# An attention and MLP kernel: h by Strassen's scheme over pairs of 384-token blocks, attention products in one group

## The chip, the core and the metric

The kernel runs on one core of a Trainium2 chip. Its engines are PE (TensorE, matrix products into PSUM), DVE (VectorE), ACT (ScalarE), POOL (GpSimd) and SP, whose queue issues every DMA here. The metric is device time in microseconds (us), the median of the runs shown.

## What is computed

Attention over 4 batches of 8 heads (576 tokens, head width 64) with a causal mask and a decay bias, then two MLPs over the 2304 tokens:

```python
attn = softmax(q @ k.T / 8 + min(-(cum_i - cum_j), 0), causal) @ v   # per batch and head
x = attn, heads side by side                       # (2304, 512)
a = x @ w1;  b = x @ w2                            # (512, 1024) each
x2 = ((a * b) @ w3) @ w_out                        # (1024, 1024), (1024, 512)
h = x2 @ w_in                                      # (512, 2048)
g = h - tanh(h)
out = g @ w_out2                                   # (2048, 512)
```

## The kernel before

Matrix products run in fp32r with every operand split into a high and a low part (`xh`, `xl`, `wih`, `wil`, ...): three matmuls (high x high, high x low, low x high) stand for one product. The split of a tile is a rounding copy (`copy`, L394 to L396, ACT or DVE) and a subtraction (`sub`, L398 to L401, DVE or POOL). The weights come as 64-bit floats in `wraw` and are put together by `assemble` (L490 to L502: one operation on ACT or DVE and four on DVE).

The program is a list of operations with the buffers that they read and write. A planner (`Plan.order`) runs this list through a model of the engines and writes the instructions of each engine in the order in which the model started them. Where an operation may run on two engines (`copy`: ACT or DVE; `sub`: DVE or POOL) it picks one. The numbers in `PARAM` are its priorities and biases, so a new `PARAM` is a new order everywhere. Engines and the SP queue run their lists strictly in order.

The stages follow each other on PE, with overlaps on the other engines:

- **Attention** (`head`, 32 heads). Scores of five query tiles into PSUM (L668 in batch 0, L670 and L671 later), the bias and row maximum on DVE (L685), the exponential on ACT (L691), transposes of the weights on PE into a ring of banks (`flip`, L725; from batch 1 on three banks, `tr_ring`), copies of these to `en`, and for a pair of heads the products with v (`pv`, L752) in two groups: query tiles 0 to 2 and tiles 3 to 4, into one bank (`pv_ring`), each followed by a copy to `xf`. `xf` is scaled by the inverse row sums (L780) and split into `xh`, `xl`.
- **Products** a and b over blocks of 512 tokens (`products`, L806), filler for PE between the heads; a times b (L815) goes to memory as `c_d`.
- **w3 times w_out** (L870 to L872), once, so that x2 needs one product.
- **x2** (L907 to L909): blocks `XT` of 512 tokens (four, and one of 256) are read back from `c_d`, split and multiplied; high and low parts go to memory as `x2_d`.
- **Last stage** (L926 to L978). For each of the five blocks `HT` and each of 16 slices f of w_in: twelve matmuls into one bank of a ring of four (h, L945), then the gate: Square, Square, Tanh, Relu on ACT (L953 to L958), four operations on DVE (L956, L957, L959, L960), a rounding copy `gh` and the residue `gl` (L401, POOL). One slice later come the output matmuls, three for each 128 tokens (L966 to L968), into four banks that collect all 16 slices. w_in is converted before the stage and stays in `wih` and `wil`.

```python
BLK = 512
HT = [(t, min(t + BLK, NT)) for t in range(0, NT, BLK)]
h_ring = Ring(bank[BLK // P:8])
s_ring.bufs, s_ring.i, tr_ring.bufs, tr_ring.i = bank[0:2], 0, bank[3:6], 0
```

## Time and profile before

| | us |
|---|---|
| median of 3 runs (930.68 to 930.79) | 930.7 |
| profiled execution | 931.5 |
| its span | 929.8 |
| busy: PE / DVE / ACT / POOL | 921.6 / 700.5 / 426.6 / 377.8 |
| attention with products, to 292 us | 292 |
| products and w3 x w_out | 142 |
| x2 | 98.5 |
| h, gate and output | 392.5 |
| tail | 4.8 |

Busy times are shares of one profiled execution. Matmuls are pipelined, and the profile models their ends: a PE that is busy throughout may still run below its rate, so the distance between the starts of matmuls is the better measure. The chain of waits follows the end of the program back from step to step; where it runs over PE, PE sets the time.

### The profile page before, as it was taken

The numbers are of one execution on the slowest core, as the hardware profiler recorded it, in microseconds if no ns is written. First come the engines' busy times: TensorE is split into PE (matmuls) and PEld (weight loads), VectorE is DVE, ScalarE is ACT, GpSimd is POOL, SyncE is SP. The second block draws the span as 40 slices with busy tenths as digits, with TensorE's granted clock in tenths as the row PEclk, the third lists the DMA queues.
The fourth block names the chain that finished last, engine by engine and source line by source line (L and its number), as shares of the span: only waits on it lengthen the run. The fifth ranks groups of instructions, "written<-read, shape, count | busy, mean of one in ns | idle before, by whom it ended". The sixth has DMA issues, their size and how long they took to land.

```text
span 929.8 us, 14217 instructions
## 1 busy us (share of the span) xinstructions
PE 921.6 (99%) x5007; PEld 765.1 (82%) x5007; DVE 700.5 (75%) x1485; ACT 426.6 (46%) x952; POOL 377.8 (41%) x309
## 2 busy tenths in 40 slices
PE   9999999999999999999999999999999999999998
PEld 7777878888887888899888988888888888888887
DVE  8999897876664299996789999997556655656665
ACT  7857565655551022211423275554444444444353
POOL 2256765545342044414978544452222222222221
PEclk9999999999999999999999999999999999999999
DMA  7666646654421144477897652221020001100010
GB/s 226 183 199 181 201 146 205 213 160 135 131 84 49 56 147 155 164 233 240 284 326 247 227 176 68 75 107 46 1 91 15 31 1 46 46 1 0 1 47 23
DMA packets 58888, 115.36 MB, mean 124 GB/s; under 512 B 5713, under 2 KB 24305, under 8 KB 58818
## 3 DMA queue, kind: packets, MB, share of 16 engines
q1 hardware_dynamic: 58818, 114.47, 38.6%
q8 instruction: 39, 0.64, 0.3%
q14 instruction: 31, 0.25, 0.1%
HBM read 85.30 MB, written 25.46 MB: 119 GB/s over the span
## 4 chain that ended last, share of the span: by engine, by line
PE 92%; DVE 4%; POOL 1%; issue 1%; ACT 1%; DMA 1%; POOLq 0%; DVEq 0%
PE bank L945 21%; PE bank L806 20%; PE bank L966 7%; PE bank L967 7%; PE bank L968 7%; PE bank L725 5%; PE bank L752 4%; PE bank L908 4%; PE bank L909 4%; PE bank L907 4%; PE bank L670 2%; PE bank L671 2%; PE bank L668 2%; PE bank L872 1%; PE bank L871 1%; PE bank L870 1%
## 5 line engine op out<-in xcount | busy, mean ns | idle before, releaser
L401 POOL TENSOR_TENSOR gl<-pg,gh 128x512 fp32r<-128x512 f32 (+1 forms) x78 | 99.2, 1272 | 260.9 <-DVE gh L396 249.0
L945 PE MATMUL bank<-x2b,wih 128*128 128x512 f32 (+1 forms) x640 | 181.3, 368 | 0.0
L945 PEld LDWEIGHTS bank<-x2b,wih 128*128 128x128 f32 x640 | 117.0, 188 | 21.2
L958 ACT ACTIVATE mk<-u,const 128x512 f32<-128x512 f32 (+1 forms) x80 | 54.5, 681 | 142.5 <-DVE pg L960 142.4
L945 PE MATMUL bank<-x2b,wil 128*128 128x512 f32 (+1 forms) x320 | 117.7, 368 | 0.0
L966 PE MATMUL bank<-voh,gh 128*128 128x512 f32 x288 | 112.2, 390 | 0.0
L967 PE MATMUL bank<-vol,gh 128*128 128x512 f32 x288 | 112.2, 390 | 0.0
L968 PE MATMUL bank<-voh,gl 128*128 128x512 f32 x288 | 112.0, 389 | 0.0
L691 ACT ACTIVATE e<-e,nmx 128x576 f32<-128x576 f32 (+4 forms) x160 | 89.2, 559 | 39.7 <-DVE nmx L685 38.8
L956 DVE TENSOR_TENSOR pg<-bank,u 128x512 f32<-128x512 f32 (+1 forms) x80 | 50.9, 636 | 42.3 <-POOL gl L401 42.3
L685 DVE CUSTOM_DVE_ANT_0 e<-bank,msk 128x288 f32<-128x288 f32 (+4 forms) x160 | 64.3, 422 | 16.5 <-PE bank L671 14.2
L725 PE MATMUL bank<-ident,e 128*128 128x128 f32 (+1 forms) x480 | 75.4, 276 | 0.6 <-ACT e L691 0.3
L396 DVE CAST gh<-pg 128x512 fp32r<-128x512 f32 (+1 forms) x77 | 30.5, 396 | 52.8 <-PE bank L967 52.6
L945 PEld LDWEIGHTS bank<-x2b,wil 128*128 128x128 f32 x320 | 60.3, 188 | 9.9
L401 POOL TENSOR_TENSOR xl<-cf,xh 128x512 fp32r<-128x512 f32 (+1 forms) x40 | 53.3, 1360 | 34.2 <-DVE xh L396 32.3
L953 ACT ACTIVATE u<-bank 128x512 f32<-128x512 f32 (+1 forms) x80 | 43.7, 546 | 50.4 <-PE bank L945 42.3
L395 ACT ACTIVATE en<-bank 128x256 f32<-128x256 f32 (+3 forms) x97 | 40.9, 427 | 52.2 <-PE bank L725 42.3
L495 ACT ACTIVATE wt<-wraw 128x512 f32<-128x512 f32 x54 | 36.4, 673 | 59.4 <-DMA wraw<-w_in 26.7
L968 PEld LDWEIGHTS bank<-voh,gl 128*128 128x128 f32 x288 | 54.1, 188 | 11.4
L966 PEld LDWEIGHTS bank<-voh,gh 128*128 128x128 f32 x288 | 54.2, 188 | 10.8
L967 PEld LDWEIGHTS bank<-vol,gh 128*128 128x128 f32 x288 | 54.1, 188 | 10.5
L806 PE MATMUL bank<-xh,w1h 128*128 128x512 f32 (+1 forms) x160 | 62.7, 392 | 0.0
(134 smaller groups left out, 2280.2 us busy)
## 6 DMA issues: line engine op xcount, KB each, us to landing
rqk<-qk SPq DMA_DIRECT2D x24, 576.0 KB
wraw<-w_out SPq DMA_DIRECT2D x24, 512.0 KB
wraw<-w SPq DMA_DIRECT2D x16, 512.0 KB
c_d<-cst SPq DMA_DIRECT2D x32, 256.0 KB
wraw<-w3t SPq DMA_DIRECT2D x16, 512.0 KB
wraw<-w_in SPq DMA_DIRECT2D x16, 512.0 KB
cf<-c_d SPq DMA_DIRECT2D x32, 256.0 KB
x_d<-x2s SPq DMA_DIRECT2D x16, 512.0 KB
```

Source lines behind the costliest of these rows:

```text
L401: o.append(("POOL", c_pool2(n), lambda: nc.gpsimd.tensor_tensor(dst(), a(), b().bitcast(F32), op=ALU.subtract)))
L685: nc.vector.tensor_tensor_reduce(e.t[:nq, EOFF[t] + k0:EOFF[t] + k1], bk.t[:nq, :k1 - k0], bi.t[:nq, bo + k0:bo + k1], -0.125, 3.0e38 if f ...
L691: act(lambda: nc.scalar.activation(et(), et(), AF.Exp, bias=nmx.t[:nq, i, tm:tm + 1], scale=-1.0, accum_out=ssum.t[:nq, pj, t, i:i + 1]), ...
L725: nc.tensor.transpose(bk.t[:rows, (at + m) * P:(at + m + 1) * P], e.t[:, EOFF[t] + c * P:EOFF[t] + c * P + rows], ident.t)
L806: nc.tensor.matmul(bk.t[:, :w], w_.t[:, k, f * P:(f + 1) * P], x_.t[:, k, :w], start=k == 0 and i == 0, stop=k == KC - 1 and i == 2)
L945: nc.tensor.matmul(bk.t[:, :w], w_.t[:, k, a], X2.t[:, i, k, :w], start=k == 0 and n == 0, stop=k == KC - 1 and n == 2)
L953: act(lambda u=u, hp=hp, c_=c_: nc.scalar.activation(c_(u), hp(), AF.Square), w, [bk], [u], pr, psum=True)
L956: dve(lambda u=u, pg=pg, hp=hp, c_=c_: nc.vector.tensor_tensor(c_(pg), hp(), c_(u), op=ALU.mult), w, [bk, u], [pg], pr)
L958: act(lambda u=u, mk=mk, c_=c_: nc.scalar.activation(c_(mk), c_(u), AF.Relu, bias=const.t[:, 1:2]), w, [u, const], [mk], pr, extra=93.0)
L966: nc.tensor.matmul(bank[n].t, gh.t[:, a], voh[f].t, start=f == 0, stop=False)
L967: nc.tensor.matmul(bank[n].t, gh.t[:, a], vol[f].t, start=False, stop=False)
L968: nc.tensor.matmul(bank[n].t, gl.t[:, a], voh[f].t, start=False, stop=f == NF2 - 1)
```

## The change

1. **h by Strassen's scheme** (Winograd's form). Tokens go in three pairs of 384-token blocks, w_in is cut into halves of its rows and of its columns. A step (one of 8 column slices, 128 columns of either half) makes the four products of the 2 x 2 scheme from seven: seven times six 384-column matmuls into two banks (three in the first pair's first step), and five additions on DVE out of these banks. m1, h11 and the rest then lie in SBUF, in the buffers `cst` and `asb`, and the gate reads them there.
2. **Its operands.** Combinations of w_in (`weights`) are made from a first conversion to memory (`wi_d`, laid by during the attention), split and written to `ws_d`; a step reads its seven of 256 kB each into a ring of 13. Combinations of x2 (`operands`) are made directly from the first two x2 blocks for the first pair, and through memory (`xf_d`, `x2_d`) for the later ones.
3. **x2** runs in six blocks of 384.
4. **Attention from batch 1 on:** both `pv` groups of a pair as one, in banks 2 and 3; the transposes have banks 4 and 5.
5. **A new `PARAM`**, and biases of its own for the planner near the end and for some kinds of operation. The output banks are six (3 x 128 tokens for two blocks).

```diff
-BLK = 512
-HT = [(t, min(t + BLK, NT)) for t in range(0, NT, BLK)]
-XT = [(t, min(t + 512, NT)) for t in range(0, NT, 512)]
+XB = 384
+XT = [(t, t + XB) for t in range(0, NT, XB)]
+NPAIR = len(XT) // 2
+NFP = NF2 // 2
+ORDER = (0, 5, 1, 6, 4, 3, 2)
...
-            s_ring.bufs, s_ring.i, tr_ring.bufs, tr_ring.i = bank[0:2], 0, bank[3:6], 0
+            s_ring.bufs, s_ring.i, tr_ring.bufs, tr_ring.i = bank[0:2], 0, bank[4:6], 0
+            pv_ring.bufs, pv_ring.i = bank[2:4], 0
...
+    for n in range(NF2):
+        c, kg, m = n // 8, n // 4 % 2, n % 4
+        j, i = ((0, 0), (0, 1), (1, 1), (1, 0))[m]
+        k, qd = j * 2 + kg, c + 2 * i
+        lay_by(wi_d, k * 4 + qd, w_in[k * P:(k + 1) * P, qd * 512:(qd + 1) * 512], PARAM["layw"] + 10 * n)
...
             if i:
-                pv(1)
+                pv([0, 1] if merged else [1])
...
+        def lay(i, x):
+            for m in range(2):
+                st = wst_r.next()
+                split(lambda st=st: st.t[:, :, 0], (st, 0), lambda st=st: st.t[:, :, 1], (st, 1),
+                      lambda m=m: v_(x).rearrange("p (f x) -> p f x", x=P)[:, m * 2:m * 2 + 2], 256, [x], pr, kind="late")
...
+            s3 = made(a11, a21)
+            lay(6, s3)
...
+        b11, b12, b21, b22 = b
+        lay(0, b11)
+        lay(1, b21)
+        lay(2, b22)
+        lay(4, made(b12, b11, b11))
+        lay(6, made(b22, b12, b12))
+        t2 = made(b22, b11)
+        lay(5, t2)
+        lay(3, made(b21, t2, b21))
...
+        def product(n, i, bk, first):
+            def mm():
+                for kg in range(2):
+                    for m, (a, z) in enumerate(((0, 0), (0, 1), (1, 0))):
+                        nc.tensor.matmul(bk.t[:, :XB], W[i].t[:, kg, a], X[i].t[:, kg, z], start=first and kg == 0 and m == 0, stop=kg == 1 and m == 2, skip_group_check=True)
...
+        def plus(bk, y):
+            x, v_ = tmp()
+            dve(lambda: nc.vector.tensor_tensor(v_(), bk.t[:, :XB], y[1](), op=ALU.add), XB, [bk, y[0]], [x], -1.0e6)
...
+        a, b = h_r[0].next(), h_r[0].next()
+        product(0, 0, a, True)
+        m1 = taken(a)
+        product(1, 5, b, True)
+        u2 = plus(b, m1)
+        product(2, 1, a, False)
+        h11 = taken(a)
+        gated(h11, fp, 0)
+        product(3, 6, b, False)
+        u3 = plus(b, m1)
+        c = h_r[0].next()
+        product(4, 4, c, True)
+        h22 = plus(c, u3)
+        gated(h22, fp + NFP, 1)
+        product(5, 3, b, False)
+        h21 = plus(b, m1)
+        gated(h21, fp + NFP, 0)
+        product(6, 2, c, False)
+        h12 = plus(c, u2)
+        gated(h12, fp, 1)
```

What this does to the order of the instructions, at three places. First PE in the last stage: L945 is h before, L966 to L968 are the output; bank_58 to bank_65 are the eight banks. Before, a stretch is twelve matmuls into one bank and twelve output matmuls:

```order
L966 MATMUL bank_59<-voh_4958,gh_4985 128x512
L967 MATMUL bank_59<-vol_4970,gh_4985 128x512
L968 MATMUL bank_59<-voh_4958,gl_4988 128x512
L945 MATMUL bank_64<-x2b_4982,wih 128x512 x2
L945 MATMUL bank_64<-x2b_4982,wil 128x512
```

In the changed kernel, L1062 is one of the seven products and L1102 to L1104 are the output:

```order
L1062 MATMUL bank_65<-x2b_4931,ws_4941 128x384 x6
L1062 MATMUL bank_64<-x2b_4932,ws_4942 128x384 x6
L1102 MATMUL bank_60<-voh_4953,gh_5401 128x512
L1103 MATMUL bank_60<-vol_4965,gh_5401 128x512
L1104 MATMUL bank_60<-voh_4953,gl_5409 128x512
L1102 MATMUL bank_61<-voh_4954,gh_5402 128x512
L1103 MATMUL bank_61<-vol_4966,gh_5402 128x512
L1104 MATMUL bank_61<-voh_4954,gl_5410 128x512
L1102 MATMUL bank_62<-voh_4954,gh_5402 128x512
L1103 MATMUL bank_62<-vol_4966,gh_5402 128x512
L1104 MATMUL bank_62<-voh_4954,gl_5410 128x512
L1062 MATMUL bank_65<-x2b_4933,ws_5383 128x384 x6
```

The products come one or two at a time between one to four output groups, and only bank_64 and bank_65 take them in turn. Second, DVE in the same stage. Before, a tile of 512 columns has five operations here, and `gl` is POOL's:

```order
L959 TENSOR_TENSOR th_4994<-bank_63,th_4994 128x512
L956 TENSOR_TENSOR pg_4995<-bank_62,u_4989 128x512
L957 SCALAR_TENSOR_TENSOR pg_4995<-sq_4991,pg_4995 128x512
L960 COPY_PREDICATED pg_4995<-mk_4997,th_4993 128x512
L396 CAST gh_4983<-pg_4996 128x512
```

In the changed kernel (L1071 are the additions out of the banks, L1085, L1091 and L1094 the gate, L414 the residue):

```order
L1071 TENSOR_TENSOR asb_104<-bank_65,asb_103 128x384
L414 TENSOR_TENSOR gl_5405<-pg_5419,gh_5397 128x384
L1071 TENSOR_TENSOR asb_105<-bank_64,cst_100 128x384
L1085 TENSOR_TENSOR pg_5420<-asb_104,u_5414 128x384
L1085 TENSOR_TENSOR th_5418<-asb_104,th_5418 128x384
L1091 SCALAR_TENSOR_TENSOR pg_5420<-sq_5416,pg_5420 128x384
L1085 TENSOR_TENSOR pg_5419<-asb_105,u_5413 128x384
L1094 COPY_PREDICATED pg_5420<-mk_5421,th_5418 128x384
```

The residue and the additions have come to DVE, the rounding copy `gh` has gone to ACT, and POOL has two operations left in the stage. Third, DVE around the first heads of batch 1, where (before) it takes the rounding copy of q and leaves the residues to POOL:

```order
L396 CAST qs_113<-rqk_106 128x576
L396 COPY en_127<-bank_63 128x3x128
L685 ISA e_122,nmx<-bank_58,msk 128x320
L685 ISA nmx 128x1
L685 ISA e_122,nmx<-bank_59,msk 128x192
```

and now:

```order
L806 TENSOR_TENSOR xf_136<-xf_136,xr 128x512
L411 COPY en_134<-bank_63 128x2x128
L411 CAST xh_93<-xf_136 128x512
L411 CAST xh_95<-xf_136 128x64
L414 TENSOR_TENSOR xl_94<-xf_136,xh_93 128x512
L414 TENSOR_TENSOR xl_96<-xf_136,xh_95 128x64
L414 TENSOR_TENSOR kl_123<-rqk_112,kh_121 64x576
L722 RECIPROCAL ssum<-ssum 128x10
L414 TENSOR_TENSOR qs_120<-rqk_113,qs_120 64x576
```

Scaling, splits and the residues of q and k of five heads, all POOL's before, stand in DVE's queue between the maxima of the scores.

## Rows read from the trace of the kernel before

**Rows 1.** The page, chain that ended last: share of the span by engine.

```profile
PE 92%; DVE 4%; POOL 1%; issue 1%; ACT 1%; DMA 1%; POOLq 0%; DVEq 0%
```

**Rows 2.** Busy us of each engine by stage, granted PE clock, DMA share, GB/s.

```profile
0.00:91.00 91.00, 87.30 (x657) 66.63 (x657) 85.99 (x262) 66.55 (x185) 38.08 (x41) 1.00 0.68 195
91.00:292.00 201.00, 200.60 (x1336) 165.01 (x1335) 149.42 (x459) 113.23 (x328) 103.48 (x92) 1.00 0.50 152
292.00:434.00 142.00, 141.90 (x710) 120.78 (x709) 108.27 (x189) 25.26 (x41) 43.17 (x31) 1.00 0.49 163
434.00:532.50 98.50, 98.50 (x487) 83.79 (x486) 81.50 (x109) 31.55 (x53) 76.40 (x56) 1.00 0.77 257
532.50:925.00 392.50, 392.50 (x1822) 328.63 (x1821) 274.49 (x467) 189.24 (x344) 116.64 (x91) 1.00 0.13 46
925.00:929.80 4.80, 0.76 (x4) 0.29 (x2) 0.85 (x2) 0.77 (x2) 0.00 (x0) 0.95 0.30 109
```

**Rows 3.** Chain of waits, last stage: start us, length us, what (matmuls of h).

```profile
561.04 2.72 PE bank L945 x12
566.48 2.72 PE bank L945 x12
...
910.50 1.43 PE bank L945 x12
```

**Rows 4.** Chain of waits around two attention products, 208 to 220 us.

```profile
208.36 1.39 PE bank L806 x6
209.76 1.13 PE bank L752 x12
210.88 0.28 PE bank L670
211.17 0.12 PE bank L671
...
218.28 1.89 PE bank L752 x20
```

**Rows 5.** Groups of instructions by form: count, busy us, mean ns, idle before.

```profile
L815 DVE TENSOR_TENSOR cst<-bank,asb 128x512 f32<-128x512 f32 x32 | 22.0, 689 | 19.2 <-PE bank L806 18.8
L815 DVE TENSOR_TENSOR cst<-bank,asb 128x256 f32<-128x256 f32 x8 | 3.4, 422 | 3.4 <-PE bank L806 3.4
L502 DVE SCALAR_TENSOR_TENSOR wt<-wraw,wt 128x512 uint32<-128x512 uint32 x72 | 61.9, 864 | 0.2
L500 DVE SCALAR_TENSOR_TENSOR wt<-wraw,wt 128x512 uint32<-128x512 uint32 x72 | 56.7, 790 | 0.4
L498 DVE TENSOR_SCALAR wt<-wt 128x512 uint32<-128x512 uint32 x72 | 50.2, 701 | 0.4
L497 DVE TENSOR_SCALAR wt<-wt 128x512 f32<-128x512 f32 x72 | 43.4, 605 | 0.6 <-ACT wt L495 0.6
L945 PEld LDWEIGHTS bank<-x2b,wih 128*128 128x128 f32 x640 | 117.0, 188 | 21.2
```

**Rows 6.** DVE and POOL in order of time: start us, us, instruction.

```profile
340.40 0.68 DVE L500 SCALAR_TENSOR_TENSOR wt<-wraw,wt 128x512 uint32<-128x512 uint32 x1
341.00 0.42 DVE L498 TENSOR_SCALAR wt<-wt 128x512 uint32<-128x512 uint32 x1
341.33 0.68 DVE L502 SCALAR_TENSOR_TENSOR wt<-wraw,wt 128x512 uint32<-128x512 uint32 x1
...
371.11 1.58 POOL L401 TENSOR_TENSOR w3l<-wt,w3h 128x512 fp32r<-128x512 f32 x1 [4.53 <-DVE w3h L396]
371.57 1.67 DVE L502 SCALAR_TENSOR_TENSOR wt<-wraw,wt 128x512 uint32<-128x512 uint32 x1
```

**Rows 7.** Chain of waits between 50 and 91 us.

```profile
61.03 1.38 POOL qs L401
...
72.25 4.83 DMA rqk<-qk
```

**Rows 8.** Busy us by 31 us windows: the one with the most DMA.

```profile
465.00:496.00 31.00, 31.00 (x138) 25.69 (x137) 26.05 (x33) 9.84 (x17) 24.28 (x18) 1.00 0.88 294
```

More of the change, by code (lines that the diff above doesn't have):

```diff
@@ new lines, in mm @@
+            def mm():
+                for bk, q0, n, lst in work:
+                    for j, (c, a, w_) in enumerate(lst):
+                        for k in range(2):
+                            nc.tensor.matmul(bk.t[k * D:(k + 1) * D, n - w_:n], V2[k].t[:, c * D:(c + 1) * D], en[k].t[:, a:a + w_],
+                                             start=j == 0, stop=j == len(lst) - 1, skip_group_check=True)
+            pe(f_pair([x[2] for w_ in work for x in w_[3]]), mm, V2 + [(en[k], parts) for k in range(2)], [w_[0] for w_ in work], p_)
@@ L757, in head @@
+            for bk, q0, n, lst in work:
+                copy(lambda q0=q0, n=n: X.t[:, q0:q0 + n], lambda bk=bk, n=n: bk.t[:, :n], n, [bk], [X], p_, psum=True)
+        merged = len(groups) == 2 and not (b == 0 and PARAM["pvm"])
         if 0 in groups:
@@ L766, in head @@
                 softmax_tile(t)
-        if 0 in groups and i:
-            pv(0)
+        if 0 in groups and i and not merged:
+            pv([0])
         if 1 in groups:
@@ L918, in tile_kernel @@
+    x_r = Ring(x2b)
+    X0 = {i: x_r.next() for i in ORDER}
+    for j in range(len(XT)):
+        x2_block(j)
+    for i in range(NPRE):
+        out_weights(i)
     cp.close()
@@ L970, in tile_kernel, with both @@
-        for n in range(w // P):
-            ob = osb_r.next()
-            for a, z in ((0, 256), (256, 512)) if t1 == NT else ((0, 512),):
-                copy(lambda ob=ob, a=a, z=z: ob.t[:, a:z], lambda n=n, a=a, z=z: bank[n].t[:, a:z], z - a, [bank[n]], [(ob, int(a > 0))] if t1 == NT else [ob], 3.0e5 + j * 160, psum=True)
-            dma(lambda t0=t0, n=n: out[t0 + n * P:t0 + (n + 1) * P, :], lambda ob=ob: ob.t, P * DM * 4, [ob], [], 0)
+            def both(o, i, a, r, w):
+                pl.op([("DVE", c_dve(XB), lambda: nc.vector.tensor_tensor(o.t, i(), a.t, op=ALU.mult if o is pg else ALU.subtract)),
+                       ("POOL", c_pool2(XB), lambda: nc.gpsimd.tensor_tensor(o.t, i(), a.t, op=ALU.mult if o is pg else ALU.subtract))], r=r, w=w, prio=pr, two=True, kind="gate")
@@ new lines, in gated, with om @@
+            act(lambda: nc.scalar.activation(mk.t, u.t, AF.Relu, bias=const.t[:, 1:2]), XB, [u, const], [mk], pr, extra=93.0)
+            both(th, h, th, [hb, th], [th])
+            dve(lambda: nc.vector.copy_predicated(pg.t, mk.t.bitcast(U32), th.t), XB, [mk, th], [pg], pr, two=True)
+            copy(lambda: gh.t, lambda: pg.t, XB, [pg], [gh], pr)
+            sub(lambda: gl.t, lambda: pg.t, lambda: gh.t, XB, [pg, gh], [gl], pr, psum=last, kind="gate")
+            for n in range(3):
+                o = bank[l * 3 + n]
+                def om(n=n, o=o):
+                    a = slice(n * P, (n + 1) * P)
+                    nc.tensor.matmul(o.t, gh.t[:, a], voh[f].t, start=fp == 0 and f == fp + l * NFP, stop=False)
+                    nc.tensor.matmul(o.t, gh.t[:, a], vol[f].t, start=False, stop=False)
+                    nc.tensor.matmul(o.t, gl.t[:, a], voh[f].t, start=False, stop=fp == NFP - 1 and f == fp + (1 - l) * NFP)
+                pe(f_op(3 * f_mm(512)), om, [gh, gl, voh[f], vol[f]], [o], 2.0e6 + pos + PARAM["outlag"] + n_tile[0] % 4 * 40 + n * 12)
```

318 lines of the change are left out of this document (197 added, 121 removed).

## The prediction, made before the changed kernel had run

> **What bounds the kernel now.** I read the chain of waits first: 92% of the span lies on PE [rows 1]. Then the busy times by stage [rows 2]: from 91 us on PE is busy without a gap and its clock is at the full 2.4 GHz level, so I checked whether "busy" means full rate. It does. In the last stage a group of twelve 512-column matmuls takes 2.72 us, and the next one follows 5.44 us later, with twelve output matmuls between them: 24 matmuls in 5.44 us, 0.2267 us each, nothing lost between groups [rows 3]. Twelve 256-column ones take 1.43 us, 0.1192 each [rows 3]. By these prices the x2 stage is 384 x 0.2267 + 96 x 0.1192 = 98.5 us, which is its window, and the last stage 768 x 0.2267 + 192 x 0.1192 (h, 197.0) + 864 x 0.2267 (output, 195.9) = 392.9 against a window of 392.5 [rows 2]. So after 91 us the time is the sum of PE's matmuls, and whatever shortens that sum shortens the kernel, unless another engine comes forward. In the first 91 us it is different: DVE is busy for 86.0 us, and the chain there runs over POOL and DMA too [rows 2, 7].
>
> **What the change takes from PE.** A 384-column matmul isn't in the trace; it lies halfway between the two that are: (0.2267 + 0.1192) / 2 = 0.1729 us. Its bounds are those two, 0.1192 and 0.2267, but both lie on one straight line of 0.42 ns a column, and I take the line.
> - **h.** Seven products instead of eight: 24 steps (3 pairs x 8) x 7 products x 6 matmuls = 1008 x 0.1729 = 174.3 us against 197.0: **-22.7**.
> - **x2** in blocks of 384: 576 x 0.1729 = 99.6 against 98.5: **+1.1**.
> - **Attention products.** Two groups of a pair of heads, of 1152 and 2048 columns, take 1.13 and 1.89 us, 0.848 ns a column, which leaves 0.15 us fixed for each; the 192-column score matmul behind such a group takes 0.28 where the next of that width takes 0.12 [rows 4]. One group instead of two saves both, 0.31 us, for 12 pairs of heads: **-3.8**, at worst 0 if the switch costs as much elsewhere.
> - The products of x with w1 and w2, the w3 stage and the 864 output matmuls stay. 552 instead of 438 of the wide products now lie among the attention; that moves 26 us from the next stage and changes no sum.
>
> Together -25.4. The profiled execution took 931.5 us: 906.1 if PE stays the bound everywhere.
>
> **What the change puts on the others.** Free of POOL, DVE starts a 512-wide two-input operation every 0.60 us, and a one-input one every 0.33 [rows 6]. For 384 columns I scale the first down by the difference of the forms, (0.689 - 0.422)/2 = 0.13 [rows 5]: 0.47 us.
> - **Last stage.** Per step DVE gets 5 additions out of the banks and 5 operations for each of four tiles (the residue gl, so far POOL's, among them): 25 x 24 = 600, with 44 more for the operands of later pairs: 644 x 0.47 = 303, and some 19 for masks and late conversions: 322 us of PE's 174.3 + 195.9 = 370. That is 87%, where it was 274.5 of 392.5, 70% [rows 2]. ACT takes over gh (five instructions a tile for four, 189 x 1.25 = 236, plus 48 drains and a fixed part for narrower tiles: some 285 of 370). POOL has two instructions left there. DVE is hidden as a sum; whether each addition is in time is the third rival.
> - **The two banks of the products.** In the order, a bank is refilled after at least one product and two output groups: 1.04 + 2 x 0.68 = 2.4 us. The drain in between needs one DVE operation of 0.56 and a hand-over on either side, about 1 us. Only in the first step do two products on one bank follow each other directly: about 1 us, once.
> - **456 groups instead of 368** (168 products, 288 outputs). Between zero, as in the last stage of before, and 0.015 us a group, as in the attention, where six wide matmuls take 1.39 instead of 1.36 [rows 4]: 0 to 7 us. The stage is the same one, so near zero; with the first step I take **+2**.
> - **DMA.** The weights of a step are seven loads of 262 kB, 1.8 MB in 15.4 us or 119 GB/s. At a change of pair seven x2b loads of 786 kB join: 9.2 MB in two steps, 298 GB/s, and the best stretch of before carried 294 [rows 8]. Each load has a step's lead, so I take 0, at most +3 at each of two changes. SP's queue is in order: a weight load stands behind writes that wait for DVE, with 13 products (28 us) of lead.
> - **Attention.** Sixteen loads of w_in are now assembled here. Up to the last softmax DVE gets 13.5 more assemblies (2 x 0.60 + 2 x 0.33, 25 us), ten residues of q and k (0.67, 7), eight of w1 and w2 (5), 12 more drains of transposes (6) and some ten others (6 to 10): about 53 us on 235 [rows 2], minus what POOL's 40 fewer instructions no longer block. The stage lengthens with its 26 us of products to about 314, so DVE is near 90%. Products of finished blocks are queued as filler, so a late head need not stop PE. The two transpose banks come round after 2.3 us (median in the order) instead of 2.8, with drains of about 1 us; I take 0.
> - **The first 91 us**, where DVE is the bound: up to head 12 it gets 16 residues and scalings that were POOL's or new, about +14 us free, and loses blocking: four DVE forms stand at 864, 790, 701 and 605 ns where rows free of POOL show 680 and 420 [rows 5, 6]. That excess is 72 x (184 + 110 + 281 + 185) = 55 us over 298 POOL operations, 0.18 us each; some 25 fewer are 5 us. Net between +9 and, since residues get shorter (0.67 against 1.38 on POOL [rows 7]), -4: I take **+3.5**.
>
> The tail of 4.8 us [rows 2] stays. 906.1 + 2 + 3.5 = 911.6 for a profiled execution; that of before is 0.8 above its median, so **911** as a median, -2.1%.
>
> **Rivals.**
> - **DVE paces the attention.** Between heads 13 and 20 the order gives DVE 66 us of free work and about 30 POOL instructions beside it (5 us): 71. PE's matmuls in the same heads come to some 70. If DVE runs a tenth behind its free rate, PE loses 7 us; if two tenths, 14. For: 94% busy in the first 91 us. Against: DVE keeps its free step in full stretches [rows 6], and filler is there. 918 to 925, say 921.
> - **Blocking goes, and the start shortens.** One DVE operation beside POOL took 1.67 us where a free one takes 0.68 [rows 6]. At 1 us for each of the 25 POOL operations that leave the first stretch, DVE gets back 25 instead of 5, and more than the 14 it takes on: the start then shortens instead of growing, by at most the 3.7 us in which PE is idle there and the 4.8 of the one load on the chain [rows 2, 7]. 906.1 + 2 - (4 to 8.5) gives medians of 899 to 903, say 901. The Trainium skill ("SBUF — State Buffer", section "SBUF: two separate sides") says that the port pair shared by VectorE and GpSimd is an exclusive lock, and that the later one is fully blocked for the whole instruction. By that rule this rival is right; the mean of 0.18 us in the rows speaks for a mild form of it.
> - **Slower: the last stage stalls on its drains.** Place: the two product banks, each refilled behind a DVE operation in a queue that is 87% full. The cover leaves 1.4 us, three queue entries. Price: 168 products x the mean lateness. From 0.15 us each (25 us) the whole gain is gone; at 0.2 it is 34 us: 940. For: four tiles at once make bursts on DVE. Against: before, PE waited nowhere in that stage, and DVE had no more room in the x2 stage (81.5 of 98.5).
> - **Slower: the clock falls.** Short waits between groups could drop PE to its 1.2 GHz level. It showed 1.00 even in the first 91 us, with its waits, and 0.95 only in the tail [rows 2]. If 25 to 40 us of matmuls ran at the low level, they would cost that much again: about 940. The Trainium skill ("TensorE: Matmul & The Clock Gate", section "A second HAM failure mode: psum-queue depth-cycling") reports just that for a kernel that cycles through PSUM banks. By that rule this rival would decide; no stage of this trace does it.
> - **The narrow products don't get cheaper.** If weight loads set the pace at 188 ns, their mean duration [rows 5], h would be 1008 x 0.188 = 189.5: 926. Against: 256-column matmuls run at 0.119 [rows 3].
>
> **How the numbers follow.** PE's sum decides, 904 to 917: 56%. DVE paces the attention: 18%. The start shortens: 13%. Drains stall: 9%. Clock: 2%. No cheaper products: 2%. Forecast 911. Leaving out both slower cases and the outer ends of the first two rivals, the range is 902 to 925. A difference under 0.2% (1.9 us) can't be told from none. The two slower cases hold 11%, of which one point lands near the old time, and so does one of DVE pacing the attention: slower 10%, same 2%, faster 88%.
>
> **What would show it.** In the profile after: twelve-matmul stretches of h at 0.173 us each (the h term); a last stage of 370 to 374 us with PE busy throughout and the clock at 1.00; x2 at 99.6 us; one attention group per pair of about 2.9 us; the end of the attention near 314 to 318 us. PE waiting for DVE's additions or gl in the last stage would make the third rival right; chain shares of DVE between 91 and 314 us the first; an earlier first wide product the second. I would be wrong from the ground up if PE's busy share in the last stage fell below 95%.

## The result, and the profile after

The changed kernel takes **921.98 us** (median of four runs, 921.13 to 924.67) against 930.69 for the kernel before beside it: a ratio of **0.9912** (95% interval 0.989 to 0.9934). Timed again on two other occasions it gave 923.09 us, ratio 0.9913 (0.9898 to 0.9928), and 921.47, ratio 0.9891 (0.9876 to 0.9905). It is faster, as forecast, but by 8.7 us instead of 19.7.

The profiled execution of after took 924.67 us, the slowest of its four, its span 922.7. These are the page's busy times, then the chain's shares:

```profile
PE 905.6 (98%) x5149; PEld 789.5 (86%) x5149; DVE 795.5 (86%) x1852; ACT 550.6 (60%) x1291; POOL 154.5 (17%) x139
PE 87%; DVE 9%; DMA 2%; issue 1%; ACT 1%; ACTq 0%; SPq 0%; DVEq 0%
```

PE is still the bound, with a smaller share of the chain than in [rows 1]. The stages, cut where they end in after (columns as in [rows 2]: stretch, its length, busy us of PE, PEld, DVE, ACT and POOL, granted clock, DMA share, GB/s): the first 91 us, the rest of the attention, the products with w3, x2, the last stage, the tail.

```profile
0.00:91.00 91.00, 86.11 (x642) 66.24 (x643) 86.88 (x273) 67.95 (x189) 5.58 (x13) 1.00 0.68 201
91.00:319.50 228.50, 226.28 (x1461) 185.31 (x1459) 211.97 (x587) 108.07 (x307) 99.71 (x84) 0.99 0.62 193
319.50:435.40 115.90, 115.90 (x606) 99.78 (x603) 104.64 (x189) 42.12 (x86) 46.42 (x40) 1.00 0.78 251
435.40:535.30 99.90, 99.90 (x578) 99.89 (x577) 63.22 (x131) 52.69 (x117) 0.00 (x0) 1.00 0.74 232
535.30:915.50 380.20, 377.40 (x1873) 338.27 (x1871) 328.74 (x674) 277.71 (x587) 2.76 (x2) 1.00 0.61 195
915.50:922.70 7.20, 0.00 (x0) 0.00 (x0) 0.00 (x0) 2.09 (x7) 0.00 (x0) 0.70 0.40 147
```

Read against the forecast, whose sum for this span is 929.8 - 25.4 + 2 + 3.5 = 909.9 us, the missing 12.8 us lie in three places:
- **The attention.** Its last matmul starts at 319.5 us instead of 291.5. Less the wide products in it at their full rate (125.1 instead of 99.3 us), 194.3 remain, where before had 192.2; forecast: 191.9. **+2.4** (the two repeats: 193.0 and 192.7, +1.1 and +0.8; three more kernels below have the same order on PE up to 679 us: 191.8, 192.9 and 193.4). So from one execution to the next this term lies between -0.1 and +2.4.
- **The last stage**, to its last output matmul: 380.2 us against 1008 x 0.1729 + 864 x 0.2267 = 370.2 and the 2 us allowed. **+8.0**.
- **The tail**: 7.2 us from the last matmul to the end, where before had 4.1 from its last matmul at 925.8. **+3.1**.

The rest is 0.7 us shorter than forecast.

Two places of the last stage show how it comes. First a steady step in the chain of waits (start us, us, what; L1062 are the products of h, L1102 to L1104 the output matmuls):

```profile
592.52 2.08 PE bank L1062 x12
594.60 0.23 PE bank L1102
594.83 0.24 PE bank L1103
595.07 0.23 PE bank L1104
...
597.37 2.10 PE bank L1062 x12
...
605.74 1.06 PE bank L1062 x6
...
608.19 0.87 PE bank L1062 x5
```

A step (seven products, twelve output groups) lasts from 592.52 to 608.19, 15.67 us. Its 78 matmuls at the full rates are 42 x 0.1733 + 36 x 0.2267 = 15.44: 0.23 us a step are lost with no gap on PE, 5.5 us in 24 steps. Matmul by matmul (start to start) the same pattern returns throughout: after a product the first nine output matmuls take 229, 234, 236, 224, 231, 236, 229, 232 and 231 ns, and if more follow these are back at 226.7; after nine outputs the first six matmuls of a product take 171, 175, 178, 185, 176 and 181 ns, the next six 173.3. Together 42 + 27 = 69 ns for going there and back.

Second the start of the stage, PE in order of time (in brackets: idle us before, and what ended it):

```profile
535.28 3.49 PE L1062 MATMUL bank<-x2b,ws 128*128 128x384 f32 x18
539.20 2.74 PE L1062 MATMUL bank<-x2b,ws 128*128 128x384 f32 x12 [0.43 <-ACT cst L410]
543.08 2.37 PE L1062 MATMUL bank<-x2b,ws 128*128 128x384 f32 x12 [1.14 <-DVE asb L1071]
546.58 3.39 PE L1062 MATMUL bank<-x2b,ws 128*128 128x384 f32 x18 [1.13 <-DMA ws<-ws_d]
549.81 0.39 PE L1102 MATMUL bank<-voh,gh 128*128 128x512 f32 x1
```

Until the first gated tile is ready PE has only products to do, the second step's among them, and it waits for drains and for weights. The 60 matmuls up to 549.81 us take 4.1 us more than 0.1733 each: 2.8 us of idle time, and 1.3 in slower matmuls around the waits. In five more executions of this order on PE the loss is 3.1 to 4.2 us.

### The profile page after: what moved, and what is told of

Its sections match the earlier page's. It is cut to its first block, busy times and chain, and to the rows that moved or that the text cites. A ratio compares the mean times of both kernels' runs of the same rounds, so it can differ in the third digit from the quotient of the medians.

```text
span 922.7 us, 15807 instructions
## 1 busy us (share of the span) xinstructions
PE 905.6 (98%) x5149; PEld 789.5 (86%) x5149; DVE 795.5 (86%) x1852; ACT 550.6 (60%) x1291; POOL 154.5 (17%) x139
## 4 chain that ended last, share of the span: by engine, by line
PE 87%; DVE 9%; DMA 2%; issue 1%; ACT 1%; ACTq 0%; SPq 0%; DVEq 0%
PE bank L832 20%; PE bank L1062 18%; PE bank L1103 7%; PE bank L1104 7%; PE bank L1102 7%; PE bank L745 5%; PE bank L775 4%; PE bank L986 2%; PE bank L985 2%; PE bank L987 2%; PE bank L690 2%; PE bank L691 2%; PE bank L688 2%; PE bank L948 2%; PE bank L949 2%; PE bank L950 2%
## 5 line engine op out<-in xcount | busy, mean ns | idle before, releaser
L1062 PE MATMUL bank<-x2b,ws 128*128 128x384 f32 x1008 | 193.2, 337 | 2.8 <-DVE asb L1071 1.1
L1062 PEld LDWEIGHTS bank<-x2b,ws 128*128 128x128 f32 x1008 | 178.8, 188 | 12.5 <-DVE asb L1071 2.9
L711 ACT ACTIVATE e<-e,nmx 64x64 f32<-64x64 f32 (+4 forms) x160 | 89.1, 558 | 70.7 <-DVE nmx L705 70.1
L1104 PE MATMUL bank<-voh,gl 128*128 128x512 f32 x288 | 113.8, 395 | 0.0
L1102 PE MATMUL bank<-voh,gh 128*128 128x512 f32 x288 | 111.9, 389 | 0.0
L705 DVE CUSTOM_DVE_ANT_0 e<-bank,msk 128x448 f32<-128x448 f32 (+4 forms) x160 | 65.0, 418 | 4.6 <-PE bank L691 3.0
L745 PEld LDWEIGHTS bank<-ident,e 128*128 128x128 f32 (+1 forms) x480 | 54.1, 131 | 15.0 <-ACT en L410 2.5
L1071 DVE TENSOR_TENSOR asb<-bank,cst 128x384 f32<-128x384 f32 x72 | 40.0, 555 | 29.1 <-PE bank L1062 28.7
L987 PE MATMUL bank<-xh,wal 128*128 128x384 f32 x192 | 64.1, 334 | 0.0
L985 PE MATMUL bank<-xh,wah 128*128 128x384 f32 x192 | 64.1, 334 | 0.0
L986 PE MATMUL bank<-xl,wah 128*128 128x384 f32 x192 | 64.1, 334 | 0.0
L1104 PEld LDWEIGHTS bank<-voh,gl 128*128 128x128 f32 x288 | 54.0, 187 | 11.5
L832 PE MATMUL bank<-xh,w2h 128*128 128x512 f32 (+1 forms) x160 | 63.3, 396 | 0.0
L1102 PEld LDWEIGHTS bank<-voh,gh 128*128 128x128 f32 x288 | 54.1, 188 | 8.6
L414 DVE TENSOR_TENSOR gl<-pg,gh 128x384 fp32r<-128x384 f32 x96 | 53.9, 561 | 8.0 <-ACT gh L410 8.0
L832 PE MATMUL bank<-xh,w2l 128*128 128x512 f32 (+1 forms) x160 | 59.9, 374 | 0.0
```

The costliest lines, as they stand in the source:

```text
L414: o = [("DVE", c_dve(n), lambda: nc.vector.tensor_tensor(dst(), a(), b().bitcast(F32), op=ALU.subtract))]
L705: nc.vector.tensor_tensor_reduce(e.t[:nq, EOFF[t] + k0:EOFF[t] + k1], bk.t[:nq, :k1 - k0], bi.t[:nq, bo + k0:bo + k1], -0.125, 3.0e38 if f ...
L711: act(lambda: nc.scalar.activation(et(), et(), AF.Exp, bias=nmx.t[:nq, i, tm:tm + 1], scale=-1.0, accum_out=ssum.t[:nq, pj, t, i:i + 1]), ...
L745: nc.tensor.transpose(bk.t[:rows, (at + m) * P:(at + m + 1) * P], e.t[:, EOFF[t] + c * P:EOFF[t] + c * P + rows], ident.t)
L832: nc.tensor.matmul(bk.t[:, :w], w_.t[:, k, f * P:(f + 1) * P], x_.t[:, k, :w], start=k == 0 and i == 0, stop=k == KC - 1 and i == 2)
L985: nc.tensor.matmul(bk.t[:, :XB], wah.t[:, f, a], ch, start=f == 0, stop=False)
```

## The experiments

The kernel before ran beside each of them, at 930.9 to 931.8 us in the median.

**The change of width, alone in the kernel before.**

```diff
-BLK = 512
+BLK = 384
```

> The kernel before, with h in blocks of 384 tokens instead of 512 and nothing else: 96 groups of twelve 384-column matmuls, each followed by nine 512-column output matmuls. No Strassen, no new drains, no new DMA. Theory A (a run of matmuls of one width that follows a run of another width starts slowly: in the trace of after nine 512-column ones after 384-column ones lose 42 ns together and the six 384-column ones that follow lose 27): the last stage takes 1152 x 0.1732 + 864 x 0.2267 = 395.4 us plus 96 x 0.069 = 6.6, so 402, and the run about 939.5. Theory B (the loss in the last stage of after comes with its many groups, its DMA or its drains, all of which are hardly changed here): 395.4 and a run of about 933.

Measured: 948.93 us, ratio 1.0183 (1.0166 to 1.02). The chain in the last stage of this kernel (L945 are the matmuls of h):

```profile
700.54 2.10 PE bank L945 x12
704.73 2.10 PE bank L945 x12
708.92 2.10 PE bank L945 x12
```

One round of twelve products and nine outputs takes 4.19 us, where 12 x 0.1733 + 9 x 0.2267 is 4.12: 0.07 lost in each round, 6.7 us in 96 of them, and the same matmuls are slow in it by the same amounts. Theory A holds; Strassen, the drains and the DMA of after aren't needed for it. The other 9 us over my 939.5 are something else: some 8 us between 586 and 626 us, of them 6.1 in waits of PE for gating operations of DVE (3.5) and for residues of w_out2 on POOL (2.6), the rest in slower matmuls around these, and a tail 1.6 us longer.

**No change of width in after.**

```diff
-nc.tensor.matmul(o.t, gh.t[:, a], voh[f].t, ...)
+nc.tensor.matmul(o.t[:, :XB], gh.t[:, a], voh[f].t[:, :XB], ...)   (all three; copies likewise)
```

> After with 384 instead of 512 output columns computed (the last 128 are filled with a copy of the first), so that every matmul of the last stage has 384 columns. Theory A (a change of width is what slows the first matmuls of a run): every output matmul takes 0.173 us, the first six of a product too, and a steady step takes 78 x 0.1732 = 13.51 us. Theory B (each new group of matmuls costs something): a step takes 13.7 or more, with the first matmuls of a run again 5 to 12 ns slower. DVE may come into the way in this kernel (13 us of work in a step), so the single matmuls decide and not the stage.

Measured (one run, 894.09 us): all 980 matmuls between 700 and 870 us take 173 or 174 ns. Steps in the chain:

```profile
742.08 2.08 PE bank L1062 x12
...
755.60 2.08 PE bank L1062 x12
...
769.12 2.08 PE bank L1062 x12
```

13.52 us a step, 78 x 0.1733, with as many groups as in after and no loss at any start. It is the change of width and not the group. (Up to 690 us PE waits 14 us in this kernel, more than half of it for DVE, which is 98% busy there, as feared.)

**The attention part alone, and undone.** First in the kernel before, then taken back in after:

```diff
-pv(0) ... pv(1);  tr_ring.bufs = bank[3:6]
+pv([0, 1] if merged else [1]);  tr_ring.bufs, pv_ring.bufs = bank[4:6], bank[2:4]
```

```diff
-merged = len(groups) == 2 and not (b == 0 and PARAM["pvm"]);  tr_ring.bufs, pv_ring.bufs = bank[4:6], bank[2:4]
+merged = False;  tr_ring.bufs, pv_ring.bufs = bank[3:6], bank[2:3]
```

> The kernel before with the attention part of the change alone: from batch 1 on one group of attention products for a pair of heads, two banks for them, two for the transposes. My price of the merge: 12 pairs x 0.31 us less, so about 927. Rival (two transpose banks or later products hold up the heads, and that is what the attention of after lost): 930 or more, with longer gaps of PE between 91 and 292 us.

Measured: 929.42 us, ratio 0.9977 (0.9966 to 0.9988), 2.0 us faster; by the profile the attention less its wide products falls from 192.2 to 189.9, by 2.3 us. That is some 60% of my 3.8, for the merge and a new order together: the wide products now stand in 124 runs instead of 86 (what a run costs comes below). PE's gaps add up to what they were (4.1 us in either), so the two banks hold nothing up. The trace shows which half of the price failed. A merged group takes 2.87 us where the two took 1.13 and 1.89 (3.02), the 0.15 of the forecast. The other 0.16, for the matmul behind, was too much: a 192-column score matmul shows 0.19 us to the next start behind a group, but 0.17 behind a transpose and 0.09 behind a wide product or another score, and 12 of the 32 groups of before have a transpose behind them.

> After with the attention part undone: two groups of attention products for a pair of heads, three transpose banks. By the price of the merge 3 to 4 us slower than after, about 925. Rival (two banks hold up the heads): not slower than after, 918 to 922, with fewer gaps of PE in the attention.

Measured: 937.04 us, ratio 1.0061 (1.0038 to 1.0083), 14 to 15 us slower than after. The direction fits the merge, the size doesn't: the attention less its wide products is 201.2 us (after: 194.3), the x2 stage is 2.7 us longer (PE waits 1.8 for xl in it) and the last one 2.1. The planner's numbers go with the merged form, and this run doesn't give a price of the merge.

**DVE relieved in the attention.** The four DVE operations on each piece of w_in are left out:

```diff
-lay_by(wi_d, k * 4 + qd, w_in[...], PARAM["layw"] + 10 * n)
+lay_raw(wi_d, k * 4 + qd, w_in[...], PARAM["layw"] + 10 * n)
```

> After without the assembly of w_in: each of its sixteen pieces is still loaded, but what is laid down for later is a copy of w1's first piece, so h is computed from other weights. That takes sixteen times two operations of 0.33 and two of 0.60 us off DVE (30 us) and 16 off ACT, nearly all before the end of the attention. Theory (DVE paces the attention of after; its PE lost 6.8 us more there than in before): the attention stage shrinks by 5 to 7 us and the run comes to 915 to 917. Rival (the clock, the merged products or the two banks cost that time): the stage keeps its length within 1.5 us and the run stays at 920 to 922.

Measured: 926.70 us, ratio 0.9947 (0.9932 to 0.9962), so no faster than after. DVE and PE between 114 and 300 us, after ahead of this run:

```profile
114.00:300.00 186.00, 186.00 (x1230) 153.02 (x1230) 177.18 (x508) 93.48 (x267) 90.53 (x75) 1.00 0.67 206
```

```profile
114.00:300.00 186.00, 186.00 (x1214) 153.20 (x1213) 146.79 (x454) 79.16 (x235) 86.10 (x75) 1.00 0.67 214
```

DVE does 30 us less and PE is full in both. The attention less its wide products stays at 192.7 us, within the range of after's repeats. A DVE that is 95% busy isn't the bound there. But this settles the stretch from 114 us on alone, where PE waits for nothing in either run. Ahead of it PE does wait. Between 60 and 200 us, after ahead of before (us in all, times, the longest):

```profile
PE bank L690 <- DVE nmx L705: 4.2, 5, 2.2
PE bank L745 <- ACT en L410: 1.4, 3, 0.7
```

```profile
PE bank L670 <- DVE nmx L685: 1.2, 2, 0.8
PE bank L725 <- ACT e L691: 0.3, 1, 0.3
```

All of after's lie between 62 and 114 us, where this run takes nothing off DVE (50.6 us busy, after 49.9) and PE waits 3.8 us for its maxima as well. So my theory falls from 114 us on; for 62 to 114 us it stays open. (Its span is 2.5 us longer than that of after, at the seam of the x2 and the last stage, which its other order made worse.)

**Work given back to POOL at the start.**

```diff
-early=102263
+early=28242
```

> After with one number of the planner as near to before as it was: the time up to which DVE is preferred for residues and copies is 28 us instead of 102 (before: 28). From 28 to about 100 us 24 more operations go to POOL, which in after does 0.3 us of work between 30 and 84 us while DVE is 99% busy there. Theory (DVE alone paces the attention up to about 84 us; PE's gaps over 0.3 us add up to 4.4 us between 60 and 80 us, 1.7 in before): those gaps fall to about 2 and the run comes to 917 to 920. Rival (POOL takes twice as long for a residue and blocks DVE beside it, so that the heads come no earlier): 921 to 925.

Measured: 942.32 us, ratio 1.0115 (1.0093 to 1.0137): 20 us slower, far beyond the rival too. DVE by form between 84 and 200 us, this run ahead of after (count, busy us, mean ns):

```profile
L522 DVE SCALAR_TENSOR_TENSOR wt<-wraw,wt 128x512 uint32<-128x512 uint32 x10 | 12.5, 1248 | 0.0
L517 DVE TENSOR_SCALAR wt<-wt 128x512 f32<-128x512 f32 x10 | 11.2, 1131 | 1.3 <-ACT wt L515 1.2
L520 DVE SCALAR_TENSOR_TENSOR wt<-wraw,wt 128x512 uint32<-128x512 uint32 x10 | 8.9, 896 | 0.0
```

```profile
L520 DVE SCALAR_TENSOR_TENSOR wt<-wraw,wt 128x512 uint32<-128x512 uint32 x13 | 10.6, 826 | 0.0
L522 DVE SCALAR_TENSOR_TENSOR wt<-wraw,wt 128x512 uint32<-128x512 uint32 x13 | 9.7, 760 | 0.0
L517 DVE TENSOR_SCALAR wt<-wt 128x512 f32<-128x512 f32 x13 | 6.4, 505 | 0.1
```

Beside 60 POOL operations these three of an assembly take 3.28 us, beside 42 they take 2.09; in after between 30 and 84 us, where POOL does two, 1.77. In 84 to 200 us DVE is as busy as in after (109 us of 116) and gets less done. PE waits 10.7 us between 62 and 200 us (after: 5.7), and 13.6 us lie at the low clock (3.4). So giving operations back to POOL doesn't help here, however full DVE is. The 20 us are the price of this whole new order; what the POOL operations alone cost in it isn't separated.

**Products in groups of six.**

```diff
-for k in range(KC):          pe(3 * f_mm(w), ...)
+for ks in ((0, 1), (2, 3)):  pe(6 * f_mm(w), ...)
```

> After with the products of x with w1 and w2 put on PE in groups of six matmuls instead of three (the same matmuls in the same banks, only the planner may not split them). In the attention of after they stand in 136 runs, 96 of them of three matmuls, before in 86 runs, 35 of three; at the start of each run its first matmul takes about 0.32 instead of 0.227 us, some 0.10 us for each run. Theory (the 50 more runs are where the attention of after lost 3.3 to 4.7 us): with some 92 runs the wide products lose 10 us instead of 14 and the run gains 3 to 4 us. Rival (a run of six holds up the short groups of the heads, which DVE waits for): the runs are fewer, but the other matmuls of the attention take as much longer, no gain or a loss.

Measured: 938.51 us, ratio 1.0071 (1.0054 to 1.0088). The runs fell from 136 to 89, the rest of the attention, its waits included, took 8.6 us longer than in the repeat of after beside it (923.09 us), and later stages waited too: the rival holds. The 0.10 us for a run, on which I had based it, was a misreading. The first wide matmul shows 0.32 us, but the transpose ahead of it shows only 0.028 to its successor's start, where it has 0.109 among its own kind. Both ends counted (what the run's matmuls take over 0.2267 us each, less what the matmul ahead of it is shorter than among its own kind), the 86 runs of before cost 4.9 us. The 136 of after cost 6.4 in its profiled execution and 5.0 in the first kernel with three tiles (below), where the clock stayed up, and the 89 of this run 5.7. That is 0.04 to 0.06 us a run, and fewer runs don't cost less.

**The start of the last stage.** Three attempts on the conversions of w_out2. First an earlier due time:

```diff
-out_weights(i)        (due 3.5e5 + 10 * i)
+out_weights(i, 2.6e5)
```

> After with the first twelve conversions of w_out2 due ahead of the last x2 blocks instead of behind them. In after they run on DVE while the first step of h starts, and PE loses 3.2 us in gaps and 0.9 in slower restarts between 535 and 550 us (waits for DVE's and ACT's drains of the product banks 1.6, for weight loads 1.1). Theory (the conversions are in the way, and their loads stand ahead of the weights on SP's queue): the gaps fall below 1 us, the run to 918 to 919. Rival (the first step waits for its own chain of drains and gating whatever DVE does): the gaps stay above 2.5 us.

Measured: 926.36 us, ratio 0.995 (0.9931 to 0.9968). PE idles 4.4 us at the start instead of 2.8, and 3.4 us lie at the low clock there. But the conversions had stayed where they were (DVE does them from 533 to 541 us as before), so this decides nothing. Then without them:

```diff
-convert(w_out2[f * P:(f + 1) * P, :], voh[f], vol[f], ...)
+dma(voh[f], wi_d[2 * f % NF2]); dma(vol[f], wi_d[(2 * f + 1) % NF2])
```

> After without the conversions of w_out2: its tiles are filled by DMA with pieces of w_in, so the output is computed from other weights. That takes 80 operations of DVE (44 us) and 32 of ACT away, all between the last x2 blocks and the first steps. Theory (the conversions hold up the first drains): PE's gaps between 533 and 550 us, 3.2 us in after, fall below 1. Rival (the first step has nothing to put between its products but the next step's, so it waits for its own drains, and for weights that can be loaded only when the memory of the x2 stage is free): 2 to 3 us of gaps remain.

Measured: 922.95 us, ratio 0.9909 (0.9895 to 0.9924). PE at the start of the stage:

```profile
537.27 5.36 PE L1064 MATMUL bank<-x2b,ws 128*128 128x384 f32 x30
543.28 6.75 PE L1064 MATMUL bank<-x2b,ws 128*128 128x384 f32 x36 [0.65 <-DVE asb L1073]
```

The loss falls from 4.1 to 1.2 us (0.7 of it idle) and the stage is 3 us shorter: the conversions were in the way. The run gains nothing, since in its new order the x2 stage is 103.6 us long instead of 99.9, with a wait of 1.5 us for xh and 3.4 us at the low clock behind it. Then four forms of assembling a part of w_out2 ahead, each with three output tiles (below), that is some 2 us better than after if nothing else moved:

```diff
-lay=0, layp=616215, layf=502811, nosb=2
+lay=8, layp=240000, layf=260000, nosb=3     (the second: lay=12)
-lay = FO[:PARAM["lay"]]
+lay = FO[-PARAM["lay"]:]                    (the third, with lay=8)
-... 3.5e5 + 10 * i)
+... 3.0e5 + (i // 2 - 2) * 160)             (the fourth, with lay=4)
```

> After with three output tiles (as in the run on the tail) and with eight of the sixteen pieces of w_out2 assembled ahead of the memory that holds them: they are laid down in DRAM during the w3 and x2 stages and only split when the last stage begins. Between the last weights and the first addition of the last stage DVE's order has 9 operations of assembly and residues instead of 46. Theory (these hold up the first drains): PE's gaps at the start of the last stage fall from 3.2 to about 1 us, nothing is lost in the x2 stage, the tail is 2 us shorter: 917.5 to 919.5. Rival (the weights for the second step come late anyway, or the x2 stage gets the wait): 920 to 922, the tail alone.

> The same with twelve pieces instead of eight: 14 operations ahead of the first addition, and one instead of twenty left for the later steps. Theory: as with eight pieces, 917 to 919.5. Rival: the earlier assembly delays the operands of the x2 stage by more than it saves, 921 or more.

> After with three output tiles, and with the last eight pieces of w_out2 in the order of use assembled ahead (before it was the first eight); the first eight are converted at the start of the last stage as in after, but the late ones need no assembly any more and are written within the first step. Theory (the cost can be saved by place): gaps at the start of the last stage below 2 us, none later, 918 to 920. Rival (it only moves): a gap of 2 us or more in the x2 stage or in the first steps, 921 or more.

> After with three output tiles, the first four pieces of w_out2 assembled ahead, and the due times of the other twelve set by the step that uses them, two steps ahead. Theory: as for the run with the last eight, 918 to 920. Rival: 921 or more.

Measured: 927.48 us (ratio 0.9966, 0.9952 to 0.9979), 931.04 (1.0007, 0.9998 to 1.0015), 933.75 (1.0027, 1.0016 to 1.0038) and 927.39 (0.9964, 0.9951 to 0.9977). In the first of them PE idles only 0.9 us at the start, as its theory says, but a piece left over comes late some seven steps on: PE waits 3.5 us for it and 2.4 in the steps just before, for gating operations, and 10.2 us lie at the low clock; in the second PE waits 9.1 us for weights that stand behind the new loads on SP's queue; in the third 14.0 us for a gated tile; in the fourth 2.2 us for operands of x2 and 3.4 for drains. None comes to its theory's time, and the first two fail otherwise than their rivals say (the first is slower than its rival's 920 to 922 too). In all four a wait stands at another place.

**The tail.** In after, the chain at the end, from the first copy out of the output banks; the last matmul ends at 915.5 us:

```profile
912.42 0.39 ACT osb L410
...
912.82 2.03 DMA out<-osb
...
914.96 0.67 ACT osb L410 x2
...
915.64 2.04 DMA out<-osb
...
917.78 0.67 ACT osb L410 x2
...
918.48 0.38 ACT osb L410
```

Six banks end close together, two tiles take them out of PSUM, and the copies wait twice for a write to DRAM; the second of these waits lies wholly behind the last matmul. The edits, in two kernels:

```diff
-ng=8, nosb=2
+ng=8, nosb=3
+ng=7, nosb=5     (the other kernel)
```

> After with three output tiles in SBUF instead of two. All six output banks are finished at the very end, where before had two; with two tiles the copies wait for the writes to DRAM of 2.0 us each, twice in a row. Theory: from the last output matmul to the end of the span it takes 7.2 us now (4.1 in before) and about 5 with three tiles; the run gains 2 us. Rival (the last writes and not the tiles set the end): no gain.

> After with three output tiles, beside after itself. Theory (each tile fewer makes the end wait for one more write of 2.0 us): 2 us under after in the median, 5.2 us from the last matmul to the end. Rival (the scatter that comes with short stretches at the 1.2 GHz level is larger than the gain): within 1 us of after.

> After with five output tiles and, to make room for them, seven instead of eight pairs of gated tiles. Theory: no copy waits for a write any more, about 4 us from the last matmul to the end, 3 us under after. Rival: the seventh pair is missed in the steady steps, and the last stage is longer by more than a microsecond.

> The changed kernel once more, unaltered, beside the two others on the same chip. The profiled run of after had 3.4 us at the 1.2 GHz level at 109.5 us, where PE had waited 2.2 us for a maximum of DVE just before. If such a stretch comes with the waits and not with the program, another run shows it elsewhere or not at all, and the times scatter by the 2 to 3 us that it costs: 920 to 925, with a median of about 921.5.

> The changed kernel unaltered, for comparison with the two others on the same chip: 921 to 924.

Measured with three tiles: 920.89 us (919.73 to 924.73), ratio 0.9903 (0.9875 to 0.9931); again, beside after, **919.94** (919.12 to 920.10), ratio **0.9871** (0.9854 to 0.9887), where after took 921.47 (921.06 to 922.24). The chain, in the first of the two:

```profile
910.30 2.04 DMA out<-osb
...
912.44 0.67 ACT osb L410 x2
...
913.13 0.67 ACT osb L410 x2
...
913.81 0.38 ACT osb L410
```

One write is gone from the chain, and 5.2 us lie behind the last matmul. The second time it is 1.5 us under after on the same chip, no run of either lies among those of the other, and it is the fastest of the kernels here that do all the work. With five tiles no write is left in the chain and the tail is 4.3 us, but the times scatter from 918.1 to 922.5 (median 920.34, ratio 0.9878, 0.9857 to 0.9898): no further gain that these runs can tell.

The two repeats of after show where some of the scatter comes from. The stretches at the low clock in three profiles, after (the second of its rows below), its second repeat, and the kernel with the last eight pieces ahead:

```profile
105.00:109.50 4.50, 2.28 (x11) 1.29 (x10) 4.50 (x7) 1.10 (x3) 2.48 (x2) 1.00 0.08 26
109.50:112.90 3.40, 3.40 (x11) 2.75 (x10) 3.22 (x11) 1.42 (x4) 0.00 (x0) 0.50 0.21 79
```

```profile
80.20:83.60 3.40, 3.17 (x10) 2.45 (x11) 2.61 (x6) 1.54 (x4) 0.00 (x0) 0.50 0.47 128
```

```profile
546.10:559.80 13.70, 3.02 (x7) 2.40 (x8) 13.50 (x27) 9.11 (x19) 0.00 (x0) 0.50 0.70 258
```

At 0.50 the clock is at its 1.2 GHz level: a 512-column matmul shows 427 ns to the next start in after's stretch instead of 227. Ahead of the first two PE had waited: 2.2 us for one of DVE's maxima in after, several waits of at most 0.7 us from 73 us on in the repeat; the last begins within a wait of 14.0 us and ends 3.0 us behind it. The first repeat has its stretch at 108.4 us, much as after, and the kernel with three tiles, in the same order up to there, none, neither time. So it comes with waits, and not in every execution. By these figures it costs some 1.7 us each time that 3.4 us of matmuls fall into it (an estimate).

## Why the forecast was right, and where it was wrong

The mechanism held: PE sets the time, and the seven products bring their gain. Three terms failed. The +2 us for the groups and the first step of the last stage measured 9.6 (5.5 and 4.1), the tail that "stays" grew by 3.1, and the attention came out within 2.4 us of its forecast only because its errors nearly cancel. Term by term:

- **h: right.** Twelve 384-column matmuls take 2.08 us, 0.1733 each, where the line through the two known widths gave 0.1729. The seven products bring what they should.
- **x2: right**, 99.9 us for a forecast of 99.6.
- **456 groups: the step that failed most.** I took them "near zero", with +2 for them and the first step together, because "the stage is the same one". But in its full blocks it never changed the width, and now does so four times there and back in a step, some of them after short runs. That costs 5.5 us (shown by the 384-token blocks in the kernel before, and by its absence with 384 output columns). The bound of 0.015 us a group, 7 us in all, held the size; my choice between the bounds was wrong. The trace of before had a better neighbour: [rows 3] ends with its one block of 256 tokens, where widths do change. I read the 0.1192 us of its products and not the six output matmuls behind them: they take 234, 235, 229, 232, 231 and 227 ns, 1.39 us instead of 1.36.
- **The first step: mis-sized.** 1 us was for two products on one bank. It is 4.1 us (2.8 idle, 1.3 in slower matmuls), because PE runs out of other work until the first tile is gated, while conversions of w_out2 stand on DVE; without them it is 1.2. I had listed these as "late conversions" in DVE's sum and not asked where they lie. Here, and only here, the third rival came true; in the steady steps PE waits for nothing, with DVE at 328.7 us of 380.2 (86%; forecast 87%) and ACT at 277.7 (forecast 285).
- **DMA: right.** No change of pair shows a wait.
- **The tail: missed.** "Stays" overlooked that the last step now ends six banks and not two, for two output tiles: 3.1 us.
- **The merge: mis-sized.** 2.0 to 2.3 us instead of 3.8, in the kernel before. The 0.15 us of a group was right, the 0.16 of the matmul behind it was too much.
- **The start: too much.** I gave it +3.5 us. The first wide product comes at 61.5 us instead of 63.2, but between 62 and 84 us PE then waits 3.5 us instead of 1.2, so that the first 91 us come out near nothing. Between 30 and 84 us DVE is busy for 53.3 instead of 51.3 us, and the four operations of an assembly take 2.18 us there instead of 3.03 (the means of after are below; L502 and L498 of before stood at 1074 and 832 ns in this stretch).

```profile
L520 DVE SCALAR_TENSOR_TENSOR wt<-wraw,wt 128x512 uint32<-128x512 uint32 x7 | 4.7, 671 | 0.0
L522 DVE SCALAR_TENSOR_TENSOR wt<-wraw,wt 128x512 uint32<-128x512 uint32 x5 | 3.4, 681 | 0.0
L517 DVE TENSOR_SCALAR wt<-wt 128x512 f32<-128x512 f32 x7 | 2.9, 415 | 0.0
L518 DVE TENSOR_SCALAR wt<-wt 128x512 uint32<-128x512 uint32 x7 | 2.9, 414 | 0.0
```

So the second rival's mechanism was there, and it ate the growth without shortening the start. The mean of 0.18 us a POOL operation, over the whole span, was too small for stretches where DVE is full: in the run with 18 more of them in 84 to 200 us, three operations of an assembly take 1.2 us more. The Trainium skill ("SBUF — State Buffer", section "SBUF: two separate sides") calls the port pair that the two engines share an exclusive lock: where DVE has two operands in SBUF or uses both pairs, whichever engine starts first holds it for its whole instruction, and the other is blocked. The traces agree in direction. In size, 1.2 us on ten assemblies are 12 us for 18 more POOL operations, an estimate of 0.7 us each where one on q or k takes 1.5; why less than its length, no run shows.
- **The wide products in the attention: missed, small.** Moving them "changes no sum" left out 50 more runs among narrower matmuls, 1.5 us in the profiled execution and 0.1 where the clock stayed up.
- **The attention as a whole: right by luck.** In the first kernel with three tiles, whose clock stayed up, it takes 191.8 us less its wide products, and 191.9 were forecast. Against before the attention products and the transposes take 4.9 us less, what the wide products lose is 1.3 more, and PE waits 3.2 us more, 4.2 of them added between 62 and 114 us, where I had the start's +3.5 and, from 91 us on, 0.
- **DVE pacing the attention: refuted from 114 us on.** Thirty us of DVE less changed nothing there. Between 62 and 114 us PE waits 4.2 us for DVE's maxima (before: 1.2 from 60 us on), and no run took work off DVE there without giving it to POOL.
- **The clock: in the small.** I asked whether 25 to 40 us would run at the low level; ahead of the tail it is one stretch of 3.4 us in some executions. The Trainium skill ("TensorE: Matmul & The Clock Gate", section "A second HAM failure mode: psum-queue depth-cycling") tells of a kernel whose clock oscillates while it cycles through PSUM banks. By that rule the last stage should show it. It doesn't: it cycles through two banks for 369 us at a granted clock of 1.00.

What stays open: why a change of width slows the matmuls behind it, which no view shows; what PE's waits for DVE between 62 and 114 us are worth; and whether the 3 to 4 us at the start of the last stage can be had by another order, since every place that was tried for the conversions made another wait.

## What to carry to other kernels

A price for a matmul holds among its own kind: where a change mixes widths on PE, look for the one block of the trace that already mixes them, and read both sides of the seam. Where a stage's inner loop gets better, price its first and its last pass by themselves: what fills PE before the first result is there, and how many results are finished at once at the end. An engine at 95% isn't thereby the bound, and one at 99% isn't helped by a neighbour that blocks it: find the stretch in which others wait for it, take work off it there, and see whether the waits change.

## What the runs showed of the hardware that was not expected

- 512-column matmuls behind 384-column ones lose 42 ns over the first nine, 384-column ones behind 512-column ones 27 ns over the first six, 512-column ones behind 256-column ones 28 ns over six; with one width throughout, no group loses anything (980 matmuls at 173 or 174 ns).
- After a wait at the start of the last stage the first 384-column matmul shows 252 to 283 ns to the next one's start, and the next few up to 185.
- The granted clock fell to 0.50 for 3.4 us behind one wait of 2.2 us or several of at most 0.7, in some executions and not in others of the same order, and for 13.7 us around a wait of 14.0.
